# Token rows by transposes, gate products in strips, and causal scores without their masked quarter

## The chip, the cores and the metric

The kernel runs on one core of a Trainium2 chip. The core has TensorE (matmuls), VectorE, ScalarE, GpSimd and SyncE, which issues most of the DMAs, and 16 DMA engines between HBM and the on-chip memory SBUF. Matmuls write to PSUM, eight banks that VectorE and ScalarE read. The metric is the device time of one execution in microseconds. The time before is 1383.82 us, the median of three runs (1382.86 to 1387.58).

In the profile PE is TensorE's matmuls, PEld its weight loads, DVE VectorE, ACT ScalarE, POOL GpSimd and SPq SyncE's DMA queue.

## The reference

Three layers stand behind each other: attention with a decay in place of a softmax, a top-1 mixture of eight experts, and a wide layer with the gate h cos(h).

```python
# q, k, v: (8 batches, 8 heads, 576 positions, 64), float32
gamma = 1.0 - 2.0 ** (-5.0 - np.arange(H))
rel = pos[:, None] - pos[None, :]
Dmat = np.where(rel >= 0, gamma[:, None, None] ** rel[None], 0.0)
x = np.matmul(q @ k.T / sqrt(64) * Dmat, v)       # then (4608 tokens, 512)

logits = x @ w_gate                               # (4608, 8)
expert_idx = np.argmax(logits, axis=1)
gate_w = softmax(logits)[np.arange(N), expert_idx]
x = gate_w * (np.maximum(x @ w1[e], 0.0) @ w2[e]) # e: the token's expert

h = x @ w_in                                      # (4608, 2048)
out = (h * np.cos(h)) @ w_out
```

## The kernel before

The order of instructions is written out by hand: each engine runs its instructions in the order in which the program issues them, and a tile's reader waits for its writer by semaphores.

**The attention stage**, near the first 178 us of the execution, goes through 40 steps: 8 batches of five chunks of a batch's positions, four of 128 and one of 64 ("full" and "half" chunks). All eight heads of a chunk are handled together. The causal decay gamma^(t-s) is split into a factor of the key, multiplied into v, and a factor of the query, multiplied into the output; earlier chunks come in through a state, the sum of k^T v. One step i of the loop (line 724) issues for TensorE:

- `scores(i)` (line 452): for each of four pairs of heads, two heads by two halves of the keys, matmuls in 64x64 tiles of the array, 16 for a full chunk. They fill the two PSUM banks `sc`; VectorE multiplies them by the causal mask into `pT` (line 466).
- `inter(i - 1)` (line 477): eight matmuls of the state `sbd` with the queries, in 64x64 tiles. The first chunk of a batch has none.
- `intra(i - 1)` (line 490): eight matmuls of `pT` with the scaled values `vs`, in 128x64 tiles, added to the same bank `xps`; VectorE multiplies the sum by the query's decay into `xt` (line 500). Then eight matmuls k^T v into `S` (line 506), in 128x64 tiles, which ScalarE copies to `sbd` (line 509).
- `rows(i - 2)` (line 511): four matmuls of 128x128 weights, `xt`, with 136 columns: an identity, which turns the output into rows of tokens, and eight columns of the gate's weights. ScalarE copies the rows (line 520), SyncE writes them to HBM (line 523), VectorE adds up the gate's columns (line 521).

Before that, in the same step, `decay(i + 1)` (line 443) scales v by the key's decay: eight ScalarE instructions, one for each head. Behind the chunks of a batch, the ranking of its tokens by expert is spread over the next steps (`route`, `place`, `spread`, `table`), on VectorE, GpSimd and a few short matmuls. Weights of the first expert are converted in the last and first chunk of a batch (lines 729 and 751). The load of chunk i + 4 (1 MB for a full one) is issued at the end of step i, behind the write of the rows on the same queue, into one of five buffers. Before the loop 13 warming matmuls run (`warm`), while the first loads are under way.

**The later stages** run the experts (lines 264 to 295 and 1056 to 1139) and then the wide layer (lines 1254 to 1403) in matmuls of 256 or 512 columns. Nothing in them is changed but the order of the rows in `w1`, which is laid out on the host.

## Time and profile before

| | |
|---|---|
| timed runs, us | 1383.82 (1382.86 to 1387.58) |
| profiled execution, us | 1377.58 |
| its span, first to last instruction, us | 1375.3 |
| TensorE matmuls busy | 1354.1 us (98%), 11234 records |
| TensorE weight loads busy | 1262.5 us (92%) |
| VectorE, ScalarE, GpSimd busy | 939.5, 757.2, 191.0 us |
| granted clock of TensorE, mean | 0.996 |
| HBM read and written | 247.24 and 51.47 MB |

The profiled execution has 2.3 us around its span, and is 6.2 us shorter than the median of the timed runs. TensorE's matmuls overlap in the records: a matmul's record lasts longer than the distance to the next one's start, so the time that a group of matmuls costs is read from the start of its first weight load to that of the next group's. A float32 matmul leaves two records of each kind, a transpose one.

### The profile page before, as it was taken

Reading aid. Unit: us, or ns where it says so; the run is one execution under the profiler, and the core shown is the slowest. Engines: PE = TensorE matmul, PEld = TensorE weight load, DVE = VectorE, ACT = ScalarE, POOL = GpSimd, SP = SyncE. Lnnn points to the kernel's source line nnn. Section 1 sums busy time; section 2 is a strip of 40 time slices with the busy share of each in tenths; the row PEclk is TensorE's granted clock in tenths of the full one; section 3 lists DMA queues with packets and bytes.
Section 4 is the critical chain, followed back from the end, with each engine's and each line's share of the span. In section 5 each row is a group of like instructions: output and inputs, shape, how many; then the busy total and the mean of one; then the engine's idle time right before and its main releaser. Section 6 shows DMA issues by size and latency. Waiting matters only on the chain.

```text
span 1375.3 us, 28314 instructions
## 1 busy us (share of the span) xinstructions
PE 1354.1 (98%) x11234; PEld 1262.5 (92%) x11234; DVE 939.5 (68%) x1928; ACT 757.2 (55%) x1687; POOL 191.0 (14%) x300
## 2 busy tenths in 40 slices
PE   7999999999999999999999999999999999999998
PEld 6888899999999999998999999999999999999997
DVE  4777865867778687847666676766767676666655
ACT  5788725444544455336556555555555555555544
POOL 4334530121211212100010100101001010010101
PEclk9999999999999999999999999999999999999999
DMA  8899626575876668976564655646455564564551
GB/s 290 320 329 346 213 61 217 180 262 183 285 246 203 211 230 268 331 275 259 176 258 164 220 190 191 220 166 249 183 192 201 194 233 161 209 226 162 196 184 57
DMA packets 72648, 300.58 MB, mean 219 GB/s; under 512 B 7748, under 2 KB 15904, under 8 KB 58560
## 3 DMA queue, kind: packets, MB, share of 16 engines
q1 hardware_dynamic: 60000, 256.18, 53.0%
q0 software_dynamic: 12512, 42.56, 8.3%
q8 instruction: 89, 1.46, 0.4%
q14 instruction: 47, 0.39, 0.1%
HBM read 247.24 MB, written 51.47 MB: 217 GB/s over the span
## 4 chain that ended last, share of the span: by engine, by line
PE 49%; issue 6%; POOL 0%; POOLq 0%; ACT 0%
PE acc L1341 25%; PE hps L1265 24%; POOL out_dram L1323 0%; POOLq L1430 0%; ACT ka L1295 0%; POOL spare L159 0%; PE acc L1352 0%; POOLq L1323 0%; ACT orow L1321 0%
## 5 line engine op out<-in xcount | busy, mean ns | idle before, releaser
L1341 PE MATMUL acc<-wunit,gh 128*128 128x512 f32 x1152 | 358.2, 392 | 0.0
L1265 PEld LDWEIGHTS hps<-far,wquad 128*128 128x128 f32 x2064 | 261.8, 191 | 8.0 <-ACTq L1239 0.7
L1265 PE MATMUL hps<-far,wquad 128*128 128x256 f32 x2064 | 266.7, 283 | 0.5 <-ACTq L1239 0.5
L1341 PEld LDWEIGHTS acc<-wunit,gh 128*128 128x128 f32 x1152 | 207.2, 189 | 36.0
L1341 PE MATMUL acc<-wunit,gl 128*128 128x512 f32 x576 | 224.3, 389 | 0.0
L274 PE MATMUL hps<-xT,wunit 128*128 128x256 f32 (+6 forms) x1536 | 209.4, 297 | 0.5 <-ACT yev L291 0.5
L274 PEld LDWEIGHTS hps<-xT,wunit 128*128 128x128 f32 x1536 | 206.7, 188 | 0.9 <-ACT yev L291 0.7
L289 PE MATMUL hps<-hh,wunit 128*128 128x256 f32 (+6 forms) x960 | 197.9, 301 | 0.0
L289 PEld LDWEIGHTS hps<-hh,wunit 128*128 128x128 f32 x960 | 155.8, 190 | 0.1
L289 PE MATMUL hps<-hl,wunit 128*128 128x256 f32 (+6 forms) x480 | 143.5, 299 | 1.4 <-DVE hl L278 1.4
L1323 POOL DMA_INDIRECT out_dram<-orow,perm x36 | 35.4, 982 | 740.3 <-DVE orow L1319 736.4
L1341 PEld LDWEIGHTS acc<-wunit,gl 128*128 128x128 f32 x576 | 108.2, 188 | 24.5 <-DVE gl L1308 0.8
L1306 ACT CAST gh<-sa 128x512 fp32r<-128x512 f32 x144 | 89.6, 622 | 72.9 <-DVE sa L1302 72.9
L1302 DVE SCALAR_TENSOR_TENSOR sa<-sa,box 128x512 f32<-128x512 f32 x144 | 99.0, 688 | 42.8 <-ACT sa L1300 41.7
L1265 PE MATMUL hps<-near,wquad 128*128 128x256 f32 x960 | 126.6, 283 | 0.0
L1265 PEld LDWEIGHTS hps<-near,wquad 128*128 128x128 f32 x960 | 123.1, 191 | 3.6
L1276 DVE TENSOR_TENSOR box<-hps,box 128x256 f32<-128x256 f32 x72 | 30.6, 424 | 136.7 <-PE hps L1265 136.5
L1308 DVE TENSOR_TENSOR gl<-sa,gh 128x512 fp32r<-128x512 f32 x144 | 98.9, 687 | 18.5 <-ACT gh L1306 12.9
L1297 DVE SCALAR_TENSOR_TENSOR sa<-box,ka 128x512 f32<-128x512 f32 x144 | 98.9, 687 | 12.4 <-ACT ka L1295 12.3
L1275 ACT COPY box<-hps 128x256 f32<-128x256 f32 x72 | 26.8, 372 | 141.3 <-PE hps L1265 132.5
L1021 DVE TENSOR_TENSOR wunit<-wst,wunit 128x512 fp32r<-128x512 f32 x112 | 75.2, 686 | 36.9 <-ACT wunit L1020 36.8
L1299 ACT ACTIVATE sa<-sa 128x512 f32<-128x512 f32 x144 | 91.2, 634 | 8.6 <-DVE sa L1297 8.6
(217 smaller groups left out, 1877.4 us busy)
## 6 DMA issues: line engine op xcount, KB each, us to landing
wquad<-ws SPq DMA_DIRECT2D x72, 1792.0 KB
wst<-in_moe_w_dram SPq DMA_DIRECT2D x64, 512.0 KB
ld<-in_full_dram SPq DMA_DIRECT2D x29, 1024.0 KB
ws<-cvo POOLq DMA_DIRECT2D x28, 512.0 KB, 3.5
xd<-xs SPq DMA_DIRECT2D x32, 256.0 KB
cvw<-in_moe_w_in_dram SPq DMA_DIRECT2D x16, 512.0 KB
cvw<-in_moe_w_out_dram SPq DMA_DIRECT2D x16, 512.0 KB
wd<-cvo POOLq DMA_DIRECT2D x16, 512.0 KB, 5.3
```

Source lines behind the costliest of these rows:

```text
L274: mm(out=ph[:, :n], lhsT=u[:, a, kc, f0:f0 + P], rhs=t[:, bq, kc, :n], start=(idx == 0), stop=(idx == 11))
L289: mm(out=py[:, :n], lhsT=u[:, w], rhs=t[:, :n], start=(fc == 0 and g == 0), stop=(fc == 7 and g == 2))
L1021: nc.vector.tensor_sub(out=u[:, 1, 2 * g + c], in0=s[:, c], in1=u[:, 0, 2 * g + c])
L1265: mm(out=o, lhsT=u[:, s, kc, a], rhs=x[:, bq, kc], start=(s in (0, 1, 2) and idx == 0), stop=(idx == 5), skip_group_check=True)
L1276: nc.vector.tensor_add(out=u2, in0=y[:, :HT], in1=p1)
L1297: nc.vector.scalar_tensor_tensor(out=sa, in0=x, scalar=INV2PI, in1=ka, op0=ALU.mult, op1=ALU.subtract)
L1299: nc.scalar.activation(out=sa, in_=sa, func=AF.Sin, scale=math.pi)
L1302: nc.vector.scalar_tensor_tensor(out=sa, in0=sa, scalar=-1.0, in1=x, op0=ALU.add, op1=ALU.mult)
L1306: nc.scalar.copy(out=gh, in_=sa)
L1308: nc.vector.tensor_sub(out=gl, in0=sa, in1=gh)
L1323: ins = nc.gpsimd.indirect_dma_start(out=out[:, :], out_offset=bass.IndirectOffsetOnAxis(ap=perm[:, k:k + 1], axis=0), in_=o, in_offset=None)
L1341: mm(out=acc2[T][c], lhsT=pair[n][:, fh, c % 2 * P:(c % 2 + 1) * P], rhs=u[:, w, fc % 4], start=(q == 0 and fh == 0 and n == 0 and w == 0) ...
```

## The change

- **Scores of a full chunk.** Keys 64 to 127 have no part in queries 0 to 63. Each matmul now covers either the early keys with all 128 queries or the late keys with the late 64 queries. The quarter that is left out stays as it was in the bank and is multiplied by zeros of the mask. Since it isn't written, the four banks are tiles of their own, cleared once (`banks`), and are handed out in turn (`next_bank`). In odd pairs of heads the two halves of the keys are swapped on the host (in k, v, the mask and the decay), so that four tiles of the array are in use together.
- **Rows.** The four matmuls with 136 columns become four strips, in which 32 columns of gate weights (8 and 24 zeros), a strip for each quarter of the 512 features, meet the output `xt`, and four transposes of `xt`. ScalarE copies the strips to `quarters` (`lts`), and a last matmul with eight columns, in `logits`, adds the four strips up while it turns them.
- **Places.** `rows(i - 2)` now stands between `scores(i)` and `inter(i - 1)`, and `logits(i - 2)` behind `intra(i - 1)`.
- **Scaling of v.** Four heads on ScalarE and four in one GpSimd instruction; for the first three chunks (`OWN`) one VectorE instruction for all eight, in their own step.
- **Start.** ScalarE's table is loaded at once; the k and q of the second chunk are loaded before the first chunk's v; the gate weights come on SyncE's queue, in the layout that the host made; six more warming matmuls stand behind the first scores.

```diff
+        banks = [ps1.tile([P, 4, P], F32, name=f"bank{i}") for i in range(4)]
+        for t in banks:
+            nc.vector.memset(t, 0.0)
+
+        def next_bank():
+            banks.append(banks.pop(0))
+            return banks[-1]
...
-            for h in range(H):
+            h0 = 0 if i < OWN else H // 2
+            for h in range(h0):
                 nc.scalar.mul(vs[:n, h], s["v"][:n, h], cc(C_GK + c * H + h, 1, n))
+            (nc.vector if i < OWN else nc.gpsimd).tensor_tensor(
+                out=vs[:n, h0:], in0=s["v"][:n, h0:],
+                in1=cc(C_GK + c * H + h0, H - h0, n).unsqueeze(2).to_broadcast([n, H - h0, D]), op=ALU.mult)
...
-            for j in range(4):
-                for g, r in ((0, 0), (1, D), (0, D), (1, 0)):
-                    if r < n:
-                        mm(out=scs[g][r:r + D, j, :n], lhsT=s["kT"][D * g:D * g + D, j, r:r + D],
-                           rhs=s["qT"][D * g:D * g + D, j, :n], start=(j == 0), stop=True, skip_group_check=True)
...
+                for j0 in (0, 2):
+                    for late in range(2):
+                        for j in (j0, j0 + 1):
+                            r = D * (j % 2 ^ late)
+                            for g in range(2):
+                                mm(out=scs[g][r:r + D, j, D * late:], lhsT=kT[D * g:D * g + D, j, r:r + D],
+                                   rhs=qT[D * g:D * g + D, j, D * late:], start=(j0 == 0 and not late), stop=True,
+                                   skip_group_check=True)
...
+            xt = xts[i % 3]
+            lt = next_bank()
+            for j in range(4):
+                mm(out=lt[32 * j:32 * j + 32, 0, :], lhsT=wgs[:, j, :], rhs=xt[:, j, :], start=True, stop=True,
+                   skip_group_check=True)
+            quarters = ap2.tile([P, P], F32, tag="lts", name="lts")
+            nc.scalar.copy(out=quarters, in_=lt[:, 0, :])
+            st[i]["lt"] = lt, quarters
+            two = next_bank()
+            for j in range(4):
+                nc.tensor.transpose(two[:, j, :], xt[:, j, :], ident)
             x = ap3.tile([P, 4, P], F32, tag="xs", name="xs")
-            for g in range(2):
-                two = ps1.tile([P, 4, P], F32, tag="sc", name="rw", bufs=4).rearrange("p (j a) t -> p j (a t)", a=2)
-                for j in range(2):
-                    mm(out=two[:, j, 0:RW], lhsT=xts[i % 3][:, 2 * g + j, :], rhs=wgi[:, 2 * g + j, :], start=(j == 0),
-                       stop=True, skip_group_check=True)
-                nc.scalar.copy(out=x[:n, 2 * g:2 * g + 2], in_=two[:n, :, 0:P])
-                nc.vector.tensor_reduce(out=lgt[b % 2][:n, c, g, :], in_=two[:n, :, P:RW].rearrange("p j e -> p e j"),
-                                        axis=AX.X, op=ALU.add)
+            nc.scalar.copy(out=x[:n], in_=two[:n])
             nc.sync.dma_start(out=xd[b * SEQ + o:b * SEQ + o + n, :], in_=x[:n].rearrange("p j t -> p (j t)"))
+
+        def logits(i):
+            b, c = steps[i]
+            lt, quarters = st[i].pop("lt")
+            mm(out=lt[:, 1, 0:E], lhsT=quarters, rhs=cc(C_EYE, E), start=True, stop=True, skip_group_check=True)
+            nc.vector.tensor_copy(out=lgt[b % 2][:, c, :], in_=lt[:, 1, 0:E])
...
             scores(i)
-            if i + 1 < NS:
+            if i < OWN:
+                decay(i)
+            if i == 0:
+                warm(NWARM // 2, blank, idle)
+            if OWN <= i + 1 < NS:
                 decay(i + 1)
-            if i == 1:
-                setup_rows()
+            if i >= 2:
+                rows(i - 2)
...
             if i >= 1:
                 inter(i - 1)
                 intra(i - 1)
+            if i >= 2:
+                logits(i - 2)
...
-            if i >= 2:
-                rows(i - 2)
```

How the instructions of TensorE stand in the third step (i = 2), before; `sc` and `rw` are PSUM banks, `xps` the output's, `S` the state's; line numbers are those of the kernel before:

```order
L462 MATMUL sc<-ld 64x128 x16
L487 MATMUL xps<-ld,sbd_136 64x128 x8
L497 MATMUL xps<-pT,vs 64x128 x8
L506 MATMUL S<-vs,ld 64x64 x8
L518 MATMUL rw<-wgi,xt_130 128x136 x4
```

And after, from the last two scores of that step to the first of the next one (its own line numbers; the `bank` tiles are the four banks):

```order
L502 MATMUL bank_145<-ld 64x64
L502 MATMUL bank_146<-ld 64x64
L559 MATMUL bank_147<-xt_129,wgs 32x128 x4
L566 MATMUL bank_148<-ct,xt_129 128x128 x4
L529 MATMUL xps<-ld,sbd_135 64x128 x8
L539 MATMUL xps<-pT,vs 64x128 x8
L548 MATMUL S<-vs,ld 64x64 x8
L574 MATMUL bank_147<-ca,lts 128x8
L502 MATMUL bank_145<-ld 64x128
```

The row products behind the state update are gone; strips and transposes stand between scores and state products, and the gate product with eight columns at the end.

The first DMAs on SyncE's queue, before (`ld` is a chunk's k, q, v and k by rows; `ca`, `ct` and `gx` are tables of constants):

```order
L438 DMA ld<-in_full_dram 128x1024
L701 DMA ca<-in_consts_dram 128x188
L438 DMA ld<-in_full_dram 128x512
L438 DMA ld<-in_full_dram 128x1024
L704 DMA gx<-in_consts_dram 128x512
L438 DMA ld<-in_full_dram 128x512
L438 DMA ld<-in_full_dram 128x1024 x2
L708 DMA ct<-in_consts_dram 128x229
L438 DMA ld<-in_full_dram 128x1024
L438 DMA ld<-in_full_dram 128x2048
```

The same after:

```order
L462 DMA ld<-in_full_dram 128x1024
L753 DMA ca<-in_consts_dram 128x324
L462 DMA ld<-in_full_dram 128x1024
L462 DMA ld<-in_full_dram 128x512 x2
L757 DMA gx<-in_consts_dram 128x512
L462 DMA ld<-in_full_dram 128x1024 x2
L760 DMA ct<-in_consts_dram 128x229
L761 DMA wgs<-in_moe_w_gate_dram 128x128
L462 DMA ld<-in_full_dram 128x1024
L462 DMA ld<-in_full_dram 128x2048
```

The second chunk's k and q moved ahead of the first chunk's v and k, the table `ca` grew by 136 columns, and the gate weights `wgs` stand ahead of the third chunk's v and of the fourth chunk.

ScalarE's first instructions, before (`vs` and `halfv` are the scaled values, `xs` the rows):

```order
L449 ACT_TABLE_LOAD
L449 ACTIVATE vs<-ld,ca 128x64 x24
L509 COPY sbd_136<-S 128x256
L449 ACTIVATE vs<-ld,ca 128x64 x8
L509 COPY sbd_137<-S 128x256
L520 COPY xs<-rw 128x256 x2
```

The same after:

```order
L751 ACT_TABLE_LOAD
L751 ACTIVATE spare<-biases 1x1
L551 COPY sbd_135<-S 128x256
L474 ACTIVATE vs<-ld,ca 128x64 x4
L562 COPY lts<-bank_147 128x128
L568 COPY xs<-bank_148 128x512
L551 COPY sbd_136<-S 128x256
```

The copy of the first state no longer stands behind the scaling of three chunks; from the fourth chunk on four scalings are left on ScalarE.

## Rows read from the trace of the kernel before

**Rows 1.** The page, busy us (share of the span) and instructions of each engine

```profile
PE 1354.1 (98%) x11234; PEld 1262.5 (92%) x11234; DVE 939.5 (68%) x1928; ACT 757.2 (55%) x1687; POOL 191.0 (14%) x300
```

**Rows 2.** TensorE's waits, whole execution: in total, times, longest us

```profile
PE sc L462 <- DMA ld<-in_full_dram: 4.0, 3, 3.4
PE xps L487 <- ACT sbd L509: 2.7, 1, 2.7
```

**Rows 3.** Stretch, length, busy us of PE to POOL, clock, DMA share, GB/s

```profile
0.00:21.22 21.22, 13.40 (x197) 10.79 (x197) 6.04 (x16) 9.84 (x36) 14.97 (x32) 0.92 0.86 295
52.00:64.00 12.00, 9.79 (x213) 8.51 (x205) 7.37 (x24) 7.96 (x33) 0.11 (x1) 1.00 0.88 306
64.00:161.39 97.39, 96.62 (x1973) 87.34 (x1974) 77.48 (x236) 79.22 (x285) 42.88 (x72) 1.00 0.91 321
178.00:1375.30 1197.30, 1187.52 (x7963) 1113.41 (x7962) 814.88 (x1542) 627.88 (x1225) 115.05 (x161) 1.00 0.59 208
```

**Rows 4.** Weight loads, step without state products: start, us, operation, count

```profile
113.64 0.86 PEld L462 LDWEIGHTS sc<-ld 64*64 64x64 f32 x32
114.68 0.85 PEld L497 LDWEIGHTS xps<-pT,vs 128*64 128x64 f32 x16 [0.17 <-issue]
...
116.16 0.99 PEld L518 LDWEIGHTS rw<-wgi,xt 128*128 128x128 f32 x8
117.29 0.32 PEld L462 LDWEIGHTS sc<-ld 64*64 64x64 f32 x12
```

**Rows 5.** Weight loads, step with state products, from 97.80 us

```profile
97.80 0.86 PEld L462 LDWEIGHTS sc<-ld 64*64 64x64 f32 x32
98.62 0.48 PEld L487 LDWEIGHTS xps<-ld,sbd 64*64 64x64 f32 x16
99.27 0.85 PEld L497 LDWEIGHTS xps<-pT,vs 128*64 128x64 f32 x16 [0.17 <-issue]
...
100.76 0.99 PEld L518 LDWEIGHTS rw<-wgi,xt 128*128 128x128 f32 x8
101.68 0.10 PEld L555 LDWEIGHTS <-ones 128*128 128x128 bf16 x1
```

**Rows 6.** Weight loads, state products of a half chunk (64 columns)

```profile
110.60 0.38 PEld L487 LDWEIGHTS xps<-ld,sbd 64*64 64x64 f32 x16
111.05 0.14 PEld L497 LDWEIGHTS xps<-halfpT,halfv 128*64 128x64 f32 x2
```

**Rows 7.** Weight loads of four transposes near 165 us

```profile
165.27 0.47 PEld L256 LDWEIGHTS xturn<-ct,xrow 128*128 128x128 f32 x4
```

**Rows 8.** Weight loads of three 40-column matmuls near 187 us

```profile
186.54 0.52 PEld L637 LDWEIGHTS lg<-rt,oh 128*128 128x128 f32 x3
```

**Rows 9.** ScalarE in the start stage

```profile
8.51 1.28 ACT L449 ACT_TABLE_LOAD   x1 [8.51 <-DMA ld<-in_full_dram]
...
18.98 2.02 ACT L449 ACTIVATE vs<-ld,ca 128x64 f32<-128x64 f32 x8 [1.01 <-DMA ld<-in_full_dram]
```

**Rows 10.** TensorE's matmuls in the start stage

```profile
9.88 1.98 PE L462 MATMUL sc<-ld 64*64 64x128 f32 x32 [3.44 <-DMA ld<-in_full_dram]
...
18.02 0.67 PE L487 MATMUL xps<-ld,sbd 64*64 64x128 f32 x16 [2.68 <-ACT sbd L509]
...
21.23 1.10 PE L462 MATMUL sc<-ld 64*64 64x128 f32 x32
```

**Rows 11.** The longest stall of the steady stage, ScalarE and TensorE

```profile
60.46 2.02 ACT L449 ACTIVATE vs<-ld,ca 128x64 f32<-128x64 f32 x8 [3.57 <-DMA ld<-in_full_dram]
60.85 0.39 PE L506 MATMUL S<-vs,ld 128*64 128x64 f32 x6 [1.67 <-issue]
```

**Rows 12.** SyncE's DMA queue: its waits, whole execution

```profile
SPq L523 <- ACT xs L520: 104.9, 38, 6.8
```

**Rows 13.** Groups of instructions, 20 to 180 us: count, busy us, mean ns

```profile
L466 DVE TENSOR_TENSOR pT<-sc,ca 128x512 f32<-128x512 f32 x58 | 37.1, 679 | 3.4 <-PE xps L497 2.0 <-PE sc L462 1.3
...
L626 POOL TENSOR_TENSOR rt<-hot,gl 128x200 fp32r<-128x200 f32 x7 | 5.0, 717 | 0.0
```

More of the change, by code (lines that the diff above doesn't have):

```diff
@@ L82, in const_table @@
     for c, (o, n) in enumerate(CH):
-        pos = (o + p)[:, None] - CENTER
+        swap = (np.arange(H) // 2 % 2 == 1) & (n == P)
+        pos = o + np.where(swap[None, :], (p[:, None] + D) % P, p[:, None]) - CENTER
         t[:, C_GK + c * H:C_GK + (c + 1) * H] = gam[None] ** (-pos)
@@ L106, in of_chunks, with swapped @@
     B, H_, S, D_ = q.shape
+    def swapped(x):
+        x = x.copy()
+        for o, n in CH[:-1]:
+            for j in range(1, H_ // 2, 2):
+                x[:, 2 * j:2 * j + 2, o:o + n] = np.roll(x[:, 2 * j:2 * j + 2, o:o + n], D, axis=2)
+        return x
+    k, v = swapped(k), swapped(v)
     def turned(x, o, n):
@@ L118, in of_chunks, with of_gate, of_first @@
     return full, np.concatenate([turned(k, o, n), turned(q, o, n)], axis=2), rows(v, o, n)
+def of_gate(w):
+    t = w.reshape(4, 2, D, E).copy()
+    t[1::2] = t[1::2, ::-1]
+    out = np.zeros((P, 4, 32), w.dtype)
+    out[:, :, :E] = t.reshape(4, P, E).transpose(1, 0, 2)
+    return out.reshape(P, 4 * 32)
+def of_first(w):
+    t = w.reshape(E, 4, 2, D, F1).copy()
+    t[:, 1::2] = t[:, 1::2, ::-1]
+    return t.reshape(E, DM, F1)
 @with_exitstack
@@ L374, in attn_moe_kernel @@
         rbase2 = ap1.tile([P, E], BF16, name="rbase2")
-        wgs = ap1.tile([P, 4, E], F32, name="wgs")
-        RW = P + E
-        wgi = ap1.tile([P, 4, RW], F32, name="wgi")
+        wgs = ap1.tile([P, 4, 32], F32, name="wgs")
         gx = ap1.tile([P, NCH, 4, P], F32, name="gx")
@@ L388, in setup_ranking @@
             nc.vector.memset(rsb, 0.0)
-        def setup_rows():
-            nc.vector.tensor_copy(out=wgi[:, 0::2, 0:P], in_=ident.unsqueeze(1).to_broadcast([P, 2, P]))
-            for a in range(2):
-                nc.vector.tensor_copy(out=wgi[:, 1::2, a * D:(a + 1) * D],
-                                      in_=ident[:, (1 - a) * D:(2 - a) * D].unsqueeze(1).to_broadcast([P, 2, D]))
-            nc.vector.tensor_copy(out=wgi[:, :, P:RW], in_=wgs)
         def decay_table(c):
@@ L411, in attn_moe_kernel @@
         for i in range(2):
-            t = ap1.tile([P, NCH, 2, E], F32, name=f"lgt{i}")
-            nc.gpsimd.memset(t, 0.0)
-            lgt.append(t)
+            lgt.append(ap1.tile([P, NCH, E], F32, name=f"lgt{i}"))
         halfv = [ap1.tile([P, H, D], F32, name=f"halfv{i}") for i in range(2)]
@@ L531, in route @@
             sh = [P, n, E]
-            L = ap2.tile(sh, F32, tag="L", name="L")
-            nc.vector.tensor_add(out=L, in0=lgt[b % 2][:, c0:c0 + n, 0, :], in1=lgt[b % 2][:, c0:c0 + n, 1, :])
+            L = lgt[b % 2][:, c0:c0 + n, :]
             mx = ap2.tile([P, n], F32, tag="mx", name="mx")
@@ L694, in attn_moe_kernel @@
         room_for["row"] = lambda e, c: ap3.tile([P, 4, P], F32, tag="xrow", name="xrow").rearrange("p j t -> p (j t)")
-        room_for["turn"] = lambda: ps1.tile([P, 4, P], F32, tag="sc", name="xturn", bufs=4)
+        room_for["turn"] = lambda: next_bank()
         room_for["hidden"] = hidden
-        room_for["bank"] = lambda: ps1.tile([P, 4, P], F32, tag="sc", name="hps", bufs=4).rearrange("p j t -> p (j t)")
+        room_for["bank"] = lambda: next_bank().rearrange("p j t -> p (j t)")
         room_for["out"] = lambda e, hf, dc: ap3.tile([P, 4, P], F32, tag="xs", name="yev").rearrange("p j t -> p (j t)")
+        nc.scalar.mul(spare, one[0:1], one[0:1])
         load(0, (0, 2))
         nc.sync.dma_start(out=ca[:, :C_TRI - C_MASK], in_=ctab[:, C_MASK:C_TRI])
+        load(1, (0, 2))
         load(0, (2, 3))
-        load(1, (0, 2))
+        load(0, (3, 4))
         nc.sync.dma_start(out=gx[:, 0].rearrange("p j t -> p (j t)"), in_=ctab[:, C_GX:])
-        load(0, (3, 4))
         load(1, (2, 4))
@@ L708, in attn_moe_kernel @@
         nc.sync.dma_start(out=ct, in_=ctab[:, :C_MASK])
+        nc.sync.dma_start(out=wgs.rearrange("p c e -> p (c e)"), in_=wg)
         load(2, (2, 4))
         load(3)
-        wgc = wg.rearrange("(c p) e -> p c e", p=P)
-        nc.gpsimd.dma_start(out=wgs[:, 0::2], in_=wgc[:, 0::2])
-        for a in range(2):
-            nc.gpsimd.dma_start(out=wgs[a * D:(a + 1) * D, 1::2], in_=wgc[(1 - a) * D:(2 - a) * D, 1::2])
         for c in range(1, NCH):
@@ L718, in attn_moe_kernel @@
         nc.vector.memset(idle, 0.0)
-        warm(NWARM, ps1.tile([P, 8, P], F32, tag="x", name="xps").rearrange("p a t -> p (a t)"), idle)
-        decay(0)
+        blank = ps1.tile([P, 8, P], F32, tag="x", name="xps").rearrange("p a t -> p (a t)")
+        warm(NWARM, blank, idle)
         wq = dict(zip((6, 7, 11, 15, 16, 21, 25, 26), [(key, g) for key in w_units(0) for g in range(2)]))
@@ L773, in attn_moe_kernel @@
                 unit_load(ap3, *wq[i])
+        rows(NS - 2)
         inter(NS - 1)
         intra(NS - 1)
-        rows(NS - 2)
+        logits(NS - 2)
         table(*waiting.pop())
```

36 lines of the change are left out of this document (26 added, 10 removed).

## The prediction

> **What bounds the kernel now.** I read the page's busy table first: TensorE is busy for 1354.1 of 1375.3 us [rows 1], so a change counts by what it does to TensorE, or to a transfer that TensorE waits for. The list of TensorE's waits shows how little is left besides: 4.0 us for the loads of k, q and v, 2.7 us once for ScalarE's copy of the state [rows 2]. The busy times by stretch put these into the attention stage, which the change touches and which ends near 178 us: TensorE idles 2.2 us between 52 and 64 us and 0.8 us between 64 and 161 us [rows 3]. The DMA engines are at 0.88 to 0.91 there, VectorE is busy 80% (77.5 of 97.4 us), and the clock is granted in full. After 178 us TensorE is busy 1187.5 of 1197.3 us on code that is not changed, so a microsecond won or lost before 178 us arrives at the end nearly whole. The question is then the length of one step of TensorE in the attention stage.
>
> **One step, read from the weight loads.** A step without the products with the state takes 117.29 - 113.64 = 3.65 us [rows 4]. In the step that starts at 97.80 the row products end where the ranking begins, at 101.68, in the same shape of array, and took 0.92 us from 100.76; in rows 4, where four-tile matmuls follow, they take 1.13. That step, with the state products, is therefore 101.68 - 97.80 + 0.21 = 4.09 us [rows 5], and eight more matmuls in four 64x64 tiles cost 4.09 - 3.65 = 0.44 us: 0.11 us for each group of four records of 128 columns (a float32 matmul leaves two records). With 64 columns the same eight take 0.45 instead of 0.65 us up to the next block [rows 5, 6]: 0.05 us less in each of four groups.
>
> So the 3.65 us hold: scores 8 x 0.11 = 0.88, value products the same 0.88 (eight pairs), state update 8 x 0.06 = 0.48, row products 0.92; sum 3.16. The other 0.49 us are the three places where the shape of the array changes (64x64 to 128x64 to 128x128 and back): 0.16 us each. The single places show it too: scores followed by matmuls of another shape take 1.04 us [rows 4], in the same shape 0.82 us [rows 5]. [...]
>
> **What the change does to a step.**
> - Scores: in a full chunk half of the groups have 64 columns: 4 x 0.05 = 0.20 us less. A half chunk's scores stay.
> - Row products, 0.92 us, go. In their place: four strips of 32 columns, which the trace doesn't show. Four tiles at once would be two groups of 0.11, 0.22 us; two at once, as in the value products, 0.44; one at once 0.92. I take 0.22, since four 64x64 tiles do run at once. Four transposes I put at four times the 0.11 of a record of 128 columns, 0.44 us; the loads of four in the trace span 0.47 [rows 7]. The new gate product over eight columns has two weight loads of full width: at least the 0.115 us between two records of the row products (0.92 / 8), at most twice the 0.17 us that a 40-column matmul with such weights takes (0.52 / 3) [rows 8]; I take 0.12, as the 136-column records are limited by their columns and still only 0.115 apart. Together 0.78 us: 0.14 less.
> - Shapes: the strips and transposes now stand between scores and state products, which were one run of 64x64 tiles, and the gate product stands alone at the end. Six changes in a step instead of three, five where the state products are missing: + 0.48 and + 0.32 us at 0.16 each. The half chunk's scores lose another 0.10, since they used to overlap with the state products behind them.
>
> Five steps of a batch: scores -0.80, contents -0.70, changes 4 x 0.48 + 0.32 + 0.10 = +2.34; sum +0.84 us. The start holds three steps; the other 37 make 7.4 batches: **+6.2 us**. With 0.10 or 0.22 us for a change of shape it is 0 or +12.4 us.
>
> **What it gives back.** At the start, step 3 begins at 21.23, after TensorE waited 2.68 us for the copy of the state [rows 10], which stood behind 2.02 us of scaling on ScalarE, itself behind a table load of 1.28 us and behind the loads of v [rows 9]. The first three chunks are now scaled by VectorE with one instruction each, and the table is loaded before anything arrives. Late next is the load of chunk 3, which landed at 18.98; ahead of it SP now sends 70 KB more constants (136 columns) and the 64 KB gate weights, 0.45 us at 295 GB/s [rows 3], so step 3 begins at about 19.4: **-1.8 us** (bounds 0 and -3). The four bank clears that now stand ahead of the warming matmuls, at most 0.7 us each as a product of the same 512 columns [rows 13], delay the first scores by up to 2.7 us; that is covered by the 3.4 us that TensorE idles before the second chunk's scores [rows 10].
>
> In the steady stage, SP's issue of the next load stands behind the write of the rows, which waited 104.9 us for their copy [rows 12]. The rows are now copied in the first half of a step, so the load goes out when its buffer is free, about 1 us earlier. Steps are also a little longer. The worst stall, 1.67 us before the state update at 60.85 while ScalarE waited 3.57 us for the same chunk [rows 11], is such a load. Of 3.0 us idle between 52 and 161 us [rows 3] I take 2.5 as gone, and 0.3 more from half-hidden waits: **-2.8 us** (bounds 0 and -4). At the end the last gate product waits for a ScalarE copy just issued: **+0.3 us**.
>
> The rest lies off the path. ScalarE loses four scalings a step, 1.0 us, and gains a small copy. GpSimd gets one product of 256 columns a step, some 0.9 us by the 0.72 us of its 200-column product [rows 13], with 42.9 of 97.4 us busy [rows 3]; the scaled values are needed about two steps later. If that cover were gone, in the steps of the ranking, it would cost up to 0.9 us a batch. VectorE swaps two short reductions for a copy. The work after 178 us gets its weights with rows in another order, at no cost.
>
> **Sum.** +6.2 - 1.8 - 2.8 + 0.3 = +1.9 us on the profiled execution's 1377.58 us. That one was faster than all three timed runs, so I put the difference on their median, 1383.82: **1385.7 us**. A measurement of this kernel tells some 0.3%, 4.15 us, from no change; +1.9 is inside.
>
> **Rivals.**
> 1. Faster: the new changes of shape are cheaper than the old. Strips and transposes both use all 128 rows, and a strip's weights are a quarter as wide. For: what a change costs includes a weight load that could not run ahead. Against: 128x64 to 128x128 also keeps the rows, and its change is one of the three that cost 0.49 us. At 0.08 us for each of the 14 new changes a batch gains 0.28 us, 2.1 us in all, and the time is 1383.82 - 2.1 - 4.3 = 1377.4.
> 2. Slower: the strips don't run four at once. Every strip streams all 128 rows, and no row of the trace has more than two such streams together. Two at once cost 0.22 us more in each of 37 steps, 8.1 us: 1393.8. One at once costs 0.70 more, 25.9 us: 1411.6. It decides from the first row product on, as a longer stay in the strips with no wait on any other engine.
> 3. The shorter columns save nothing, because records can't start closer together: 32 loads in 0.86 us are 27 ns apart [rows 5]. Then 0.20 us return in 29 full chunks, 5.8 us: 1391.5. Against it: the 64-column products start 16 loads in 0.38 us, the last one's 0.14 us included, 16 ns apart [rows 6]. [...]
> 4. A new wait: the strips need the scaled output right behind the next scores, where the row products had the whole step. VectorE at 80% and its 0.68 us for such a product [rows 13] could be late by up to 0.3 us in 29 steps: up to 8.7 us, 1394. Against it: the scores' masks now have 0.9 us longer until the value products, so VectorE comes to the output less late.
>
> **Chances.** Near my sum (1380 to 1388) 0.48; rival 1 or a larger gain at the start 0.24; rival 2 0.14; rival 3 0.06; rival 4 0.08. Faster by over 0.3%: 0.24; within: 0.48; slower: 0.28. The range 1376 to 1397 leaves out strips one at a time and gains beyond rival 1.
>
> **What will show it.** In the profile after, a full step with state products should last some 4.2 us instead of 4.09, a half chunk's step about 4.05 instead of 3.66; the strips should take 0.22 us and about 0.16 us more on each side; the scores should be 0.20 us shorter in their slot; step 3 should start near 19.4 us; and the idle stretch at 52 to 64 us should be mostly gone. I am wrong if a full step falls clearly under 4.0 us (changes of shape cheap), if the strips take 0.4 us or more, or if TensorE waits for VectorE or ScalarE in every step.

## The result, and the profile after

The changed kernel takes 1390.03 us (median of 5 runs, 1387.41 to 1392.64), the kernel before 1382.86 us beside it (5 runs, 1380.55 to 1387.58): ratio 1.0058, 95% interval 1.0032 to 1.0085. It is slower by 7.2 us. The forecast was 1385.7 us, its range holds the time, but its likeliest case, a difference within 0.3%, did not come.

The profiled execution after took 1391.07 us (span 1389.3), 13.5 us more than the profiled one of before. As the medians differ by 7.2 only, both kernels were profiled a second time (e7 and e8 below). The stretches, from the starts of TensorE's records, in us:

| Stretch | before | before again | after | after again |
|---|---|---|---|---|
| start to step 3's scores | 21.22 | 20.76 | 19.45 | 20.44 |
| steps 3 to 38 | 144.69 | 143.53 | 147.73 | 149.68 |
| step 39 to layer 1's first load | 7.94 | 7.73 | 11.01 | 9.47 |
| to the first output product | 436.69 | 441.05 | 443.92 | 441.91 |
| to the end of the span | 764.76 | 764.83 | 767.19 | 767.00 |
| span | 1375.3 | 1377.9 | 1389.3 | 1388.5 |

The start gained 0.3 to 1.8 us; the steps lost 3.0 to 6.2, the end of the attention stage 1.7 to 3.1, and the expert stage, which the prediction took as unchanged, 3.0 to 9.7 us.

The page's busy line of the kernel after, answering to [rows 1]:

```profile
PE 1361.6 (98%) x11480; PEld 1257.1 (90%) x11480; DVE 939.9 (68%) x1882; ACT 719.5 (52%) x1516; POOL 210.8 (15%) x332
```

Busy times by stretch of the kernel after (length; busy us of PE, PEld, DVE, ACT, POOL; clock, DMA share, GB/s), answering to [rows 3]:

```profile
0.00:21.22 21.22, 13.60 (x253) 10.65 (x253) 10.36 (x22) 5.12 (x15) 13.86 (x29) 1.00 0.91 313
52.00:64.00 12.00, 12.00 (x275) 10.09 (x269) 9.79 (x26) 6.25 (x21) 4.32 (x7) 1.00 0.90 310
64.00:161.39 97.39, 95.92 (x2046) 79.35 (x2044) 73.26 (x198) 55.43 (x179) 54.15 (x91) 0.98 0.89 308
161.39:178.00 16.61, 14.77 (x266) 12.27 (x261) 10.54 (x36) 6.95 (x19) 10.74 (x22) 0.90 0.15 58
178.00:1389.30 1211.30, 1195.11 (x8004) 1119.51 (x8003) 816.64 (x1548) 628.34 (x1228) 114.26 (x161) 1.00 0.58 205
```

The idle stretch at 52 to 64 us is gone, as predicted, but that can't be put down to the change: in the second profile of before (e7) TensorE idles there for 0.2 us only. TensorE now idles 1.5 us between 64 and 161 us (0.8 before) and 1.8 us up to 178. The loads of TensorE's weights in an undisturbed step with the state products, answering to [rows 5] (start, us, operation, count, idle before):

```profile
102.38 0.76 PEld L502 LDWEIGHTS bank<-ld 64*64 64x64 f32 x32
103.21 0.16 PEld L559 LDWEIGHTS bank<-xt,wgs 128*32 128x32 f32 x8
103.56 0.42 PEld L566 LDWEIGHTS bank<-ct,xt 128*128 128x128 f32 x4 [0.20 <-ACT halfv L474]
104.15 0.43 PEld L529 LDWEIGHTS xps<-ld,sbd 64*64 64x64 f32 x16 [0.17 <-ACT lts L562]
104.75 0.85 PEld L539 LDWEIGHTS xps<-pT,vs 128*64 128x64 f32 x16 [0.17 <-issue]
105.57 0.60 PEld L548 LDWEIGHTS S<-vs,ld 128*64 128x64 f32 x16
106.24 0.30 PEld L574 LDWEIGHTS bank<-ca,lts 128*128 128x128 f32 x2
106.56 0.48 PEld L491 LDWEIGHTS bank<-ld 64*64 64x64 f32 x13
```

From start to start: scores 0.83 us, strips 0.35, transposes 0.59, state products 0.60, value products 0.82, state update 0.67, gate product 0.32; 4.18 in all, where the prediction had "some 4.2" and before 4.08. The eight loads of the four strips lie within 0.16 us, and their products start in two groups of four, 7 ns apart within a group and 0.13 us from the first group to the second, so the strips run together. Undisturbed steps by the chunk whose scores they hold, 0 to 4: before 3.84, 3.65, 4.24, 4.08, 3.66 (a batch 19.47), after 3.84, 3.58, 4.35, 4.17, 3.96 (19.90).

The start, TensorE's products, answering to [rows 10]: step 3 begins at 19.46, but only after the gate product waited for a copy that ScalarE holds behind a scaling, which waits for a load (TensorE, and below it ScalarE).

```profile
19.14 0.39 PE L574 MATMUL bank<-ca,lts 128*128 128x8 f32 x2 [2.27 <-ACT lts L562]
19.46 0.90 PE L502 MATMUL bank<-ld 64*64 64x128 f32 x32
```

```profile
17.88 1.06 ACT L474 ACTIVATE vs<-ld,ca 128x64 f32<-128x64 f32 x4 [5.99 <-DMA ld<-in_full_dram]
18.85 0.24 ACT L562 COPY lts<-bank 128x128 f32<-128x128 f32 x1
```

The longest pause of the steady stage, TensorE's products and below them ScalarE's scaling, answering to [rows 11]:

```profile
91.57 0.39 PE L539 MATMUL xps<-halfpT,halfv 128*64 128x64 f32 x6 [1.40 <-issue]
91.89 0.39 PE L574 MATMUL bank<-ca,lts 128*128 128x8 f32 x2
92.14 0.89 PE L688 MATMUL lg<-rt,oh 128*128 128x120 f32 x5
92.95 1.50 PE L502 MATMUL bank<-ld 64*64 64x128 f32 x32
```

```profile
91.56 1.06 ACT L474 ACTIVATE vs<-ld,ca 128x64 f32<-128x64 f32 x4 [1.26 <-DMA ld<-in_full_dram]
```

It stands in the middle of a row of 16 value products, with nothing that they wait for, and behind it the scores take 1.50 instead of 0.90 us: the granted clock is 0.5 for 3.4 us, from 93.1 us on. At the end of the stage, TensorE, and below it VectorE:

```profile
167.80 0.43 PE L559 MATMUL bank<-xt,wgs 128*32 128x128 f32 x8
170.07 0.66 PE L566 MATMUL bank<-ct,xt 128*128 128x128 f32 x4 [1.84 <-DVE xT L288]
170.65 0.67 PE L529 MATMUL xps<-ld,sbd 64*64 64x128 f32 x16
171.25 1.70 PE L539 MATMUL xps<-pT,vs 128*64 128x128 f32 x16
```

```profile
166.81 0.17 DVE L575 COPY lgt<-bank 128x8 f32<-128x8 f32 x1
167.01 0.17 DVE L586 TENSOR_REDUCE mx<-lgt 128x2 f32<-128x16 f32 x1
...
169.11 0.30 DVE L675 TENSOR_TENSOR gl<-gts,gh 128x5 fp32r<-128x5 f32 x1
169.33 0.68 DVE L288 TENSOR_TENSOR xT<-bank,xT 128x512 fp32r<-128x512 f32 x1
```

The transposes need the bank that the first half's turned rows hold until VectorE has subtracted them (L288), and that subtraction stands behind eleven instructions of the ranking, 2.3 us. Before, the row products stood late enough in the step to wait 0.56 us only. In the first profile the granted clock then fell to 0.5 for 3.4 us, from 171.6 us on (value products 1.70 instead of 1.09 us), in the second it stayed at 1.00: 11.01 and 9.47 us for the same stretch.

### The profile page after: what moved, and what is told of

It is laid out like the page before. It is cut to its first block, busy times and chain, and to the rows that moved or that the text cites. A ratio compares the mean times of both kernels' runs of the same rounds, so it can differ in the third digit from the quotient of the medians.

```text
span 1389.3 us, 28681 instructions
## 1 busy us (share of the span) xinstructions
PE 1361.6 (98%) x11480; PEld 1257.1 (90%) x11480; DVE 939.9 (68%) x1882; ACT 719.5 (52%) x1516; POOL 210.8 (15%) x332
## 4 chain that ended last, share of the span: by engine, by line
PE 48%; issue 6%; DMA 1%; POOL 0%; POOLq 0%; ACT 0%
PE acc L1396 25%; PE hps L1320 23%; DMA wquad<-ws 1%; POOL out_dram L1378 0%; POOLq L1487 0%; ACT ka L1350 0%; POOL spare L187 0%; POOLq L1378 0%; ACT orow L1376 0%
## 5 line engine op out<-in xcount | busy, mean ns | idle before, releaser
L302 PE MATMUL hps<-xT,wunit 128*128 128x256 f32 (+6 forms) x1440 | 197.4, 298 | 1.7 <-DVE hl L306 1.3
L302 PEld LDWEIGHTS hps<-xT,wunit 128*128 128x128 f32 x1440 | 195.2, 188 | 2.4 <-DVE hl L306 1.7
```

What stands on the lines that cost most here:

```text
L302: mm(out=ph[:, :n], lhsT=u[:, a, kc, f0:f0 + P], rhs=t[:, bq, kc, :n], start=(idx == 0), stop=(idx == 11))
```

## The experiments

Each ratio is to the kernel before, timed beside it on the same chip (medians 1379.97 to 1380.71 us).

**e1, rows late.** The strips, the transposes and the gate product behind the state update.

```diff
-            if i >= 2:
-                rows(i - 2)
...
             if i >= 1:
                 inter(i - 1)
                 intra(i - 1)
             if i >= 2:
+                rows(i - 2)
                 logits(i - 2)
...
```

> The changed kernel with strips, transposes and gate product moved back to the end of a step, behind the state update, the gate product right behind the transposes. Scores and state products are one run of 64x64 tiles again: four changes of the array's shape in a step instead of six. Theory (changes of shape set the step): a full step with state products falls from 4.17 us (trace of the changed kernel) to 3.87, worked out from the slots of the two traces as scores 0.62, state products 0.65, values 0.82, state update 0.67, strips 0.35, transposes 0.44, gate product 0.32; without state products from 3.58 to 3.44, the half chunk's from 3.96 to 3.64. In 37 steps some 10 us less than the changed kernel, about 1380 against 1390, a little faster than the kernel before unless loads or code come too late. Rival (changes are cheap, the new place only brought waits for other engines at the end of the stage): steps stay within 0.1 us of 4.17 and the time falls by 2 us at most.

Measured 1389.44 us, ratio 1.0070 (1.0047 to 1.0092). The undisturbed steps did shrink, to 3.77, 3.45, 4.06, 3.88, 3.67. Of six changes of the array's shape in a step two are gone (scores and state products are one run again, transposes and gate product too), and a step of chunk 2, 3 or 4 lost 0.29 us: 0.145 us for a change, if all of it is put down to the two. But 11 us of waits ate the gain, so the theory's 1380 us did not come. TensorE's waits in e1 (us in total, times, longest):

```profile
PE bank L574 <- ACT lts L562: 4.7, 3, 3.4
PE xps L539 <- issue: 3.0, 3, 1.4
PE S L548 <- issue: 1.4, 1, 1.4
PE bank L566 <- issue: 1.3, 1, 1.3
PE xps L529 <- issue: 0.6, 1, 0.6
```

The first is the gate product, too close behind its copy. The "issue" pauses have no releaser. They became clear by numbering PE's records (loads, products, semaphore instructions) from the start: in e1 the six pauses stand at 1217, 2753, 3009, 3777, 4033 and 5569, in the kernel before the one at 60.85 us [rows 11] at 1985, in the kernel after the one at 91.57 at 3521. Each leaves 193 when divided by 256. The DMA packets show why. On the queue "instruction" q8 the kernel before has 89 packets and the kernel after 91, of 16,384 bytes each, about one for 256 of TensorE's records (22663 and 23122). The pages have, before and after (packets, MB, share of 16 engines):

```profile
q8 instruction: 89, 1.46, 0.4%
q8 instruction: 91, 1.49, 0.4%
```

The packet for the block at 1985 in the kernel before began at 58.27 us, 6.2 us after TensorE had entered the block ahead of it, and was through at 59.35; TensorE, idle since 59.18, went on at 60.85. In the kernel after the packet for 3521 was through at 90.25, and TensorE went on at 91.57. So it is with every pause of 0.4 us or more between TensorE's products that has no releaser, from 22 to 600 us in all runs: the first instruction behind it leaves 193, and its block's packet was through 1.3 to 1.6 us before. So TensorE's code comes in blocks of 256 here, one packet for 255 and 254 records in the mean, and where the next block was late, TensorE stopped. The distances over 0.35 us from one weight load to the next at such a place, 22 to 600 us (how many, and their sum):

```
before, again            1: 1.95 us    2: 2.20 us
start alone (e5)         0
cut alone (e4)           6: 3.85       cut and start (e6)         2: 1.13
after, again             4: 3.28       6: 4.98
rows late (e1)           6: 8.50       rows late, repaired (e12)  2: 3.59
turn first (e2)          2: 1.23       full scores (e3)           1: 1.11
30 products (e9)         3: 1.77       both (e10)                 2: 1.08
```

**e2, turned rows first.** In the last two steps the first half's transposes are emitted ahead of the ranking.

```diff
+            if i >= NS - 2:
+                x_block(0, i - NS + 2)
             to_spread, placed[:] = placed[:], []
...
-            if i >= NS - 2:
-                x_block(0, i - NS + 2)
```

> The changed kernel with the turning of the first expert's rows (the last two steps of the attention stage) issued ahead of the ranking, so that VectorE's subtraction that frees its bank stands ahead of the ranking's eleven short instructions. Theory (the transposes of step 39 wait 1.84 us for that bank, since the row products took another place in the round of four banks): this wait goes, step 39 starts its transposes some 2 us earlier, the time falls by about 2 us, by up to 3.5 if TensorE's clock stays up after it. Rival (VectorE is late anyhow and the wait reappears at the half chunk's mask or at the ranking): less than 0.7 us.

Measured 1386.80 us, ratio 1.0054 (1.0033 to 1.0075). In the trace, VectorE's subtraction and the transposes that wait for it:

```profile
166.21 0.69 DVE L288 TENSOR_TENSOR xT<-bank,xT 128x512 fp32r<-128x512 f32 x1 [0.94 <-ACT xT L287]
```

```profile
166.96 0.66 PE L566 MATMUL bank<-ct,xt 128*128 128x128 f32 x4 [0.44 <-DVE xT L288]
```

The wait fell from 1.84 to 0.44 us, and the stretch from step 39 to layer 1 took 8.04 us, as before (7.73 to 7.94). So the end of the stage is explained. The 1.4 us can't be told from the ratio alone.

**e3, full scores.** All scores over 128 queries, the rest as after (the extra products land in the masked quarter).

```diff
-   mm(out=scs[g][r:r + D, j, D * late:], lhsT=..., rhs=qT[..., j, D * late:], ...
+   mm(out=scs[g][r:r + D, j, :], lhsT=..., rhs=qT[..., j, :], ...
```

> The changed kernel with all scores over 128 queries, the masked quarter too, nothing else changed. Theory (a group of four records of 64 columns is 0.05 us shorter than one of 128): each full chunk's scores take 0.20 us more, 0.83 becomes 1.03 us from scores to strips, and the time rises by 5.8 us to about 1396. Rival (records can't start closer, so the shorter columns never saved anything): the slot stays at 0.83 and the time within 1 us of the changed kernel's.

Measured 1393.95 us, ratio 1.0105 (1.0083 to 1.0126). Steps of 4.05, 3.78, 4.55, 4.38, 3.96: 0.20 us more in every full chunk and nothing in the half one. The loads of one step, scores and strips:

```profile
116.00 0.86 PEld L502 LDWEIGHTS bank<-ld 64*64 64x64 f32 x32
117.04 0.16 PEld L559 LDWEIGHTS bank<-xt,wgs 128*32 128x32 f32 x8 [0.17 <-issue]
```

1.04 us between these starts, as in [rows 4], against 0.83 above. Rival 3 of the prediction falls.

**e4, the cut alone.** The kernel before with the scores, the swapped halves and the cleared banks of the change; start, rows and gate products as before.

```diff
-                for g, r in ((0, 0), (1, D), (0, D), (1, 0)):
-                    if r < n:
-                        mm(out=scs[g][r:r + D, j, :n], lhsT=..., rhs=s["qT"][D * g:D * g + D, j, :n], ...
...
+                    for late in range(2):
+                        for j in (j0, j0 + 1):
+                            r = D * (j % 2 ^ late)
+                            for g in range(2):
+                                mm(out=scs[g][r:r + D, j, D * late:], lhsT=..., rhs=qT[..., j, D * late:], ...
```

> The kernel before with the masked quarter left out of the scores (swapped halves, four banks cleared once) and nothing else of the change. Theory: 0.20 us less in each full chunk's scores, steps of 4.08 and 3.65 us become 3.88 and 3.45, 5.8 us less in 29 steps, about 1377 to 1378 against 1383, less what the loads give back: the steps come closer to the rate of the loads, which may return 2 us. Rival (no gain in the scores): as the kernel before within 1 us.

Measured 1378.61 us, ratio 0.9988 (0.9973 to 1.0002). Steps of 3.64, 3.44, 4.04, 3.88, 3.66, again 0.20 us less in full chunks; step 3 came 2 us later (23.18 us), as the four clears held up the warming products (a wait of 3.4 us for VectorE, 1.15 before), and late blocks of code took 3.85 us. So the time fell by 1.8 us only, and its interval holds no change; the theory had 3.8 to 5.8.

**e5, the start alone; e6, the cut and the start.** The changed order of the first loads, the early table load, the scaling by VectorE in three steps and the six products more, on the kernel before and on e4 (there with the clears behind the idle block's memset).

```diff
+        nc.scalar.mul(spare, one[0:1], one[0:1])
         load(0, (0, 2))
...
+        load(1, (0, 2))
         load(0, (2, 3))
-        load(1, (0, 2))
+        load(0, (3, 4))
...
+            if i < OWN:
+                nc.vector.tensor_tensor(out=vs[:n], in0=s["v"][:n], in1=..., op=ALU.mult)
```

> The kernel before with the changed start alone: the loads of chunk 1 asked ahead of chunk 0's second half, ScalarE's table load ahead of the first copy, v times decay on VectorE for the first three chunks, six more idle products behind the first scores. Theory (the start gains 1.8 us and the gain stays): step 3's scores at 19.4 to 19.7 instead of 21.22, the steps behind it at 3.84, 3.65, 4.24, 4.08, 3.66 as before, layer 1 of the first half 1.5 to 2 us earlier than 173.85, the time some 1.8 us under the kernel before: ratio 0.9987. Rival (given back): the loads of later chunks land no earlier, so the steps up to 64 us stretch by as much and step 15 starts where it did (70.9 us less 0.5 at most): ratio 1.000.

> The kernel before with the masked quarter cut, halves swapped and cleared banks (the kernel of e4) and the changed start, the four clears behind the idle block's memset; rows, gate products and the rest as before. Theory (each part's price adds up, rows are what costs): step 3 at 19.3 to 19.7 (23.18 with the cut alone), steps of 3.64, 3.44, 4.04, 3.88, 3.66 with about 0.4 us more where PE waits for GpSimd's row, layer 1 at 168 to 169 (171.7 with the cut alone), time 1374 to 1376, ratio 0.996; against the changed kernel 13 us less, so the row contents by strips and transposes with the end of the stage cost more than the whole difference. Rival (the pace is set by loads, so time saved in the steps comes back as waits): step 39 at 163.5 or later, the time as with the cut alone, 1378.6, ratio 0.999.

e5: 1377.34 us, ratio 0.9991 (0.9974 to 1.0007), step 3 at 20.18. The direction is the theory's, the size can't be told from nothing. Step 15 began at 67.85 us (70.19 and 68.93 in the two profiles of before), so the gain was not given back by then. e6: 1376.57 us, ratio 0.9978 (0.9962 to 0.9994): the fastest version here, ahead of both kernels. Step 3 came at 19.70, at the edge of the theory's, layer 1 at 166.43, earlier than its 168 to 169; the time is 0.6 us above its 1374 to 1376. Step 39 at 158.69 speaks against the rival. Part of the cut is lost in the step of chunk 0, which takes 4.1 us in most batches instead of 3.64 (GpSimd, then TensorE):

```profile
85.48 0.76 POOL L661 TENSOR_TENSOR rt<-hot,gh 128x200 fp32r<-128x200 f32 x1
86.21 0.52 POOL L661 TENSOR_TENSOR rt<-hot,gl 128x200 fp32r<-128x200 f32 x1
```

```profile
86.78 0.91 PE L672 MATMUL lg<-rt,oh 128*128 128x120 f32 x5 [0.45 <-POOL rt L661]
```

**e7 and e8, both kernels again.**

> The kernel before, unchanged, a second profiled execution. Theory (its first profile, 1377.6 us, was a short one, and the expert stage differs from execution to execution): from layer 1's first load (173.85) to the end of the span it took 1201.5 us in the first; 1203 to 1208 here, with other places of the waits and of the 3.4 us stretches at half clock. Rival (the stage always takes this, and what the changed kernel loses there is the change's): 1201 to 1202 again.

> The changed kernel, unchanged, a second profiled execution. Theory: the pauses at steps 20 and 21 (3.2 us) and part of the 9 us more in the expert stage belong to its first execution and not to the kernel: step 3 at 19.4 to 20.4, undisturbed steps of 3.84, 3.58, 4.35, 4.18, 3.96, the wait of step 39's transposes for VectorE's xT there again (1.5 to 2.5 us) with the half clock behind it, layer 1 of the first half 2.5 to 3.5 us later behind step 39 than before (7.94 us there), and from layer 1 to the end 1203 to 1209 us instead of 1211.1. Rival: the same pauses at the same steps, and 1211 again.

e7: 1380.11 us; layer 1 to the end 1205.9 us against 1201.5. e8: 1390.27 us; 1208.9 against 1211.1. So the first profile of before was a short one, as supposed. The pauses are only in part those of one execution: the longest of the first profile of after, at instruction 3521 in step 20, stands in e8 too, shorter, and the longest of e8 is at 4033 in step 23. The wait of the transposes, 1.84 us, stands in both, but in e8 the granted clock stayed at 1.00 behind it, and layer 1 came 1.5 us later than in the first profile of before, not 2.5 to 3.5. But from layer 1 to the end the five executions with the new rows (the kernel after twice, e1, e2, e3) took 1208.6 to 1211.1 us, mean 1209.5, and the five with the old rows (before twice, e4, e5, e6) 1201.5 to 1206.1, mean 1204.0: the ranges don't meet. TensorE's first output product, behind its branch over code for an overflow that doesn't occur, in the kernel after, in e8 and in e7:

```profile
622.15 3.11 PE L1320 MATMUL hps<-far,wquad 128*128 128x256 f32 x24 [0.75 <-PEq L1294]
```

```profile
621.53 4.60 PE L1320 MATMUL hps<-far,wquad 128*128 128x256 f32 x24 [3.14 <-PEq L1294]
```

```profile
613.08 3.14 PE L1265 MATMUL hps<-far,wquad 128*128 128x256 f32 x24 [0.49 <-ACTq L1239]
```

The releaser "PEq" is PE's own sequencer, in the branch. Its record in the trace, with the number of PE's records ahead of it:

```
before, again                      13071   0.45, 0.45 us
start / cut / cut and start        13081 / 13070 / 13083   0.36, 0.36, 0.36
after, again                       13530   2.57, 4.97
rows late / turn first / full      13530   4.05, 4.23, 3.63
30 products (e9), e10, e12         13650   0.36, 0.36, 0.36
before and 230 products (e11)      13991   4.55
```

**e9, e10, e11: the place of the branch.** Small products at the start, where TensorE waits anyway (3.4 us in the kernel after), move all of its code; e10 has the edit of e2 as well, e11 is the kernel before with 230 of them.

```diff
+        for _ in range(30):
+            mm(out=blank[0:1, 0:1], lhsT=one, rhs=one, start=True, stop=True)
         warm(NWARM, blank, idle)
```

> The changed kernel with 30 products of one column by one row more on TensorE, ahead of the idle products at the start, where PE waits anyway (3.38 us). They move PE's branch over the overflow code by 60 instructions. In the ten profiled executions so far that branch took PE 0.36 to 0.45 us in the five of kernels with 13070 to 13083 PE instructions ahead of it and 2.57 to 4.97 us in the five with 13530. Theory (where the branch's target lies in PE's program decides whether its code is there in time; 13590 is 13078 and 512): the branch takes 0.36 to 0.45 us, PE's wait ahead of the first product of L1320 falls from 0.75 to 3.1 us to 0.5, the expert stage from layer 1's first load to the end from 1208.6 to 1211.1 us to 1205 to 1208, the time some 3 us under the changed kernel: ratio 1.003 to 1.004. Rival (the branch takes long because something else in the new rows makes its code late): 2.5 to 5 us again, ratio 1.0058. Start and steps as in the changed kernel by both.

> The changed kernel with both repairs: the first half's transposes ahead of the ranking in the last two steps (as e2), and the 30 small products ahead of the idle ones (as e9). Theory (the losses outside the steps are the end of the stage, 3 us, and the branch, 2 to 4 us, and they add): layer 1 of the first half some 8 us behind step 39 as before, the branch at 0.4 us, time 1382 to 1384 where the kernel before has 1380, ratio 1.002; what stays is the steps' 0.43 us per batch and the pauses. Rival (the losses are hidden by a later wait, so that only one shows): ratio 1.004 to 1.0055.

> The kernel before with 230 of the same small products ahead of its idle ones: 460 PE instructions more, so that the branch lies at 13531, where it lies in the changed kernel. They delay the first scores, so its time isn't to be compared; the branch's is. Theory (the place in the program decides): 2.5 to 5 us for the branch, with PE waiting 0.7 to 3 us ahead of the first product behind it, in the kernel that took 0.45. Rival (the new rows make it long): 0.45 again.

A float32 product of this shape left two loads and two products, so 30 of them are 120 instructions and 230 are 920, not 60 and 460; the places were 13650 and 13991. e9: 1384.92 us, ratio 1.0021 (1.0004 to 1.0037), better than the theory's; layer 1 to the end 1205.8 us. e10: 1381.86 us, ratio 1.0015 (1.0000 to 1.0031), near the theory's 1382 to 1384 us; 1203.7 us. e11: the branch took 4.55 us in code that otherwise takes 0.45. The first output product in e9 and in e11:

```profile
614.68 3.14 PE L1322 MATMUL hps<-far,wquad 128*128 128x256 f32 x24 [0.49 <-ACTq L1296]
```

```profile
620.12 4.25 PE L1268 MATMUL hps<-far,wquad 128*128 128x256 f32 x24 [2.71 <-PEq L1242]
```

The theory holds on both sides: the place in the program decides, not the rows. With 0.49 us of wait in e7 the 24 products run at a granted clock of 1.00 (3.14 us); behind a wait of 3.14 us in e8 they took 4.60 us, with a mean granted clock of 0.83 from 620 to 630 us, and behind one of 2.71 us in e11 4.25 us. In each of the six slow branches one 16,384-byte packet of code began inside the branch, 0.2 to 2.6 us after its start, and the branch ended 1.41 to 1.47 us after that packet was through; in the eight quick ones none did. Counted from the last block's start, the branch was quick at 77 to 90 and at 145, slow at 25 and at 230. Why just there no run shows, nor whether 512 instructions more bring the same place again, as e9's theory took it. e9 against the kernel after is 0.37% or 5.1 us; the two weren't timed beside each other, and their intervals leave 1 to 9. From layer 1 to the end the three kernels with the shift (e9, e10, e12) took 1204.8 us in the mean, 4.7 less than the five without it: most of what the new rows lost there. Of that, 0.3 to 2.7 us (1.6 in the mean) are the idle time ahead of the first output product and up to 1.5 the clock behind it; e9 also had fewer code pauses in the steps. How much of the rest is the shift and how much chance was not settled: e11, with the slow branch and the old rows, took 1206.1 us, as much as the longest execution of the old rows without it.

**e12, rows late, repaired.** The edits of e1, e2 and e9 together.

> The changed kernel with the rows' strips and transposes moved behind the value products and the state update (as e1), the transposes of the first half ahead of the ranking (as e2), and 30 small products more at the start (as e9). In e1 an undisturbed batch took 18.78 us instead of 19.90, but six pauses of 8.5 us in all, each at a PE instruction whose number leaves 193 when divided by 256, took the gain back. Theory (such a pause is a block of code that comes late, and which blocks come late hangs on where they meet the loads, so it is not bound to the shorter steps): steps of 3.77, 3.45, 4.06, 3.88, 3.67 as in e1, 1 to 3 us of such pauses, the branch at 0.4 us, the wait for ScalarE's copy in the start there as in e1 (3.35 us), time 1376 to 1380, ratio 0.997 to 1.000. Rival (the stage can't go faster than its loads and code arrive, so shorter steps only wait longer): 7 to 9 us of such pauses again, step 39 at 169 or later, ratio 1.002 to 1.004, no better than e10.

Measured 1381.64 us, ratio 1.0002 (0.9985 to 1.0019), just above the theory's 0.997 to 1.000. The code pauses fell from 8.5 to 3.6 us, a little more than the theory's 1 to 3 and far from the rival's 7 to 9; the branch took 0.36 us. What stays is the gate product's wait:

```profile
PE bank L574 <- ACT lts L562: 5.2, 3, 3.1
```

## Why the prediction was right and wrong

- **Bound.** That TensorE's path sets the time was right. That "the work after 178 us" is "not changed" failed: its instructions are the same, but 459 more ahead of them moved its code, the branch became 2.1 to 4.5 us longer, and the stage took 5.4 us more in the mean of the five executions on each side. The branch is shown to be part of that: between layer 1's first load and the first output product TensorE idled 8.8 us with the new rows, 5.6 with the old and 5.5 with the shift, and 1.6 of the 3.2 us more stand at the branch. No row of before shows it; that a branch over other code stands there could have been asked.
- **Scores, -0.20 us in a full chunk.** Right: 0.20 to 0.21 in e3 and e4. Rival 3 is out.
- **Row contents and shapes, +0.84 us in a batch.** The mechanism was right, the term too large: +0.43, so +3.2 us in 7.4 batches instead of +6.2. Strips, transposes and gate product take 1.26 us where the row products took 1.13. Four strips run at once: 0.35 us less 0.145 for the change of shape is about the 0.22 taken; rival 2 is out. Full steps with state products came out at +0.11 and +0.09 where the term had +0.14. It was mis-sized at two places: in the step of chunk 0 (+0.14 predicted, 0.00 measured) the gate product is followed by the ranking's products in the same shape and takes 0.22 instead of 0.32 us, and the half chunk's step grew by 0.30, not 0.44. A change of shape costs 0.145 us (e1), near the 0.16 taken, far from rival 1's 0.08.
- **Start, -1.8 us.** Seen in one pair of profiles (-1.77) and hardly in the other (-0.32); e5's -0.9 in 1000 is no measurable gain. What was late next was not only chunk 3's load, but the new gate product behind ScalarE's copy, 2.3 us, which the prediction did not see.
- **Stalls, -2.8 us.** This step failed. The prediction read the 1.67 us at 60.85 [rows 11] as a wait for the load, since ScalarE waited for one at that time. It is a late block of code: its packet was through at 59.35 us (shown at e1). Whether the loads of v make it late, by sharing the DMA engines, was not shown. Such pauses did not go with the earlier issue of loads: 1.95 and 2.20 us before, 3.28 and 4.98 after. Nor can the change be blamed for more of them: with the rows in the place that they have after (also e2, e3, e9, e10) they took 2.2 us in the mean, with the old rows (also e4, e5, e6) 1.8.
- **End, +0.3 us.** Failed: +1.7 to +3.1. The prediction looked at the gate product and not at the bank that the transposes now take earlier in the step, while VectorE is in the ranking (e2).
- **Rival 4.** No wait of the strips for VectorE stands in the lists of waits after.

By terms as measured, in means of the executions: +3.2 for the steps, +2.1 for code pauses (4.1 against 2.1), -1.0 for the start, +2.4 for the end, +5.4 for the expert stage; sum +12. The two pairs of profiles have 14.0 and 10.6 between their spans, the timed runs 7.2 with 4.4 to 11.8 as their interval, so the sum is at its upper end and the terms from few executions are too large by some, the code pauses above all. In the forecast's +1.9, 3 us too many for the shapes stood against the losses not seen. That the range held the time is in part luck: the expert stage's share had no term in the sum, and the end's had 0.3 us where 2.4 came.

What stays open: TensorE's waits for VectorE's xT near 300 us and for an output weight near 637 us come and go between executions of one kernel, and were not traced further.

## What to carry to other kernels

Number the engine's instructions before you give a wait a cause: pauses "<-issue" at numbers with one and the same remainder were late blocks of code here, and loads issued earlier did not remove them. More instructions ahead of a branch made that branch slow here, far from the edit (2.57 and 4.97 us instead of 0.45); dummy products where the engine idles anyway showed it (4.55 us in e11) and mended it (0.36 us in e9). Of a change made of several parts, run the parts alone: here the cut and the start together win 0.22%, and the whole change, with the new rows, loses 0.58%.

## What the runs showed of the hardware

- TensorE's code arrived by DMA in packets of 16,384 bytes, about one for 256 records (89 for 22663, 91 for 23122). Every pause of 0.4 us or more between its products without a releaser, 22 to 600 us, ended at an instruction number with remainder 193 by 256, 1.3 to 1.6 us behind the end of its block's packet, with the DMA engines at 0.7 to 1.0 of their time.
- The same taken branch cost TensorE 0.36 to 0.45 or 2.57 to 4.97 us, by its place in the program alone (e9, e11). In the slow ones a packet of code began inside the branch, and the branch ended 1.41 to 1.47 us after it was through.
- Four 128x32 strips of float32 run at once: eight loads within 0.16 us, products 7 ns apart in groups of four, 0.35 us with the change of shape behind them.
- A float32 product of one column left two loads and two products in the trace (60 of each for 30).
